# A gated linear attention kernel: two neighbouring tokens in one partition for q, k and v, and half-size TensorE tiles inside a chunk

## The chip, the core and the metric

The kernel runs on one core of a Trainium2 chip. Its time is the device time of one execution in microseconds (us). Before the change three runs took 190.23 to 192.36 us, with a median of 191.33.

## What is computed

Inputs are q, k, v and a complex gate a = a_re + i a_im, each of 4 batches, 8 heads, 768 steps and 48 channels in 32-bit floats. In every head a complex state S of 48 x 48 is carried over the steps, and the result goes through a small two-layer network with a residual:

```python
mag = np.sqrt(a_re * a_re + a_im * a_im)
a_n = a * np.minimum(mag, 0.999) / (mag + 1e-06)     # complex
for t in range(768):
    S = a_n[t][:, None] * S + k[t][:, None] * v[t][None, :]
    y[t] = q[t] @ S.real
x  = y of all 8 heads side by side                   # (4, 768, 384)
xn = (x - mean) / sqrt(var + 1e-6) * g_ln
out = x + relu(xn @ w_ch1) @ w_ch2                   # 384 -> 1536 -> 384
```

## The kernel before

The steps of a batch are cut into chunks of 128. Two neighbouring chunks are a pair; there are 3 pairs a batch and 12 in all (P = 0 to 11, chunk n = 2P + c). Only the first pair (PARTS) is worked on in two parts of four heads each, to start sooner.

For each pair the gates give decays and phases. ScalarE takes ln of a_re (`ln`), its reciprocal (`iv`), VectorE or GpSimd the ratio a_im / a_re (`r`), its square (`r2`); then ln(1 + r2) (`u`), the log magnitude (`l`), its cap (`lc`), and arctan of the ratio (`th`). TensorE sums log magnitudes and phases over the steps with triangular matrices (`dec` L477, `ph` L492/L496), ScalarE makes exponentials (`e`, `en`) and sines and cosines (`sin`, `cos`; `qt` or `abs` give the quarter turn). So k is divided and q multiplied by the running decay (`ke`, `qe`), and each is turned by the phase (`ks`, `qs`, with the cosine part in channels 0 to 47 and the sine part in 64 to 111 of 128).

Then, in each chunk and for each of the 8 heads:

- `kT`, `qT` (L594): transposes of ks and qs, on TensorE with a copy to SBUF (`ksT`, `qsT`), or as a DMA transpose on the SP queue (L599), as the plan says.
- `am` (L617): the scores, `ksT` times `qsT`, 128 x 128; `atm` masks them on VectorE.
- `gm` (L645, with the carried state in L641): ks times v is added to the state; `G` reads it out.
- `y` (L667, L670): masked scores times v, plus qs times the state before the chunk. `x` copies it out of PSUM.

The network follows: `xtr`/`xT` transpose x (L688), `mm1` (L722) multiplies with w_ch1 in six groups a pair, `relu` (L739, L741) reads them out, `mm2` (L754) multiplies with w_ch2, `oa` (L760) and `ot` (L767, L770) scale by 1/std and add x, `st` (L777) stores. The mean and g_ln are folded into w_ch1 at the start (`wp`, `wc`, L388).

In DRAM a chunk's q, k and v lie with one step in a partition, so each packet of a load is one head's 48 channels, 192 bytes (L404). The gates lie with two neighbouring steps in a partition, 384 bytes a packet (L445):

```python
in_=ap[b].rearrange("h (c p) d -> p c h d", p=C)[:, pp * R + c]               # q, k, v: one chunk
in_=ap[b][hs].rearrange("h (k p j) d -> p k h (j d)", p=C, j=R)[:, pp]        # gates: one pair
```

The order of the work is written out: a string PLAN lists every step with its engine (P TensorE, A ScalarE, V VectorE, G GpSimd, S the SP queue) and PSUM bank, and each engine takes its own in that order. An `@` makes a GpSimd step wait for a named VectorE step. `warm` (L787) are 134 matmuls without use that fill the time in which TensorE would wait in the beginning. `tab` are the loads of ScalarE's function tables.

Of the kernel before, what the change touches and what calls it, by code (L numbers as in the profile page):

```python
# [34 lines left out]

ENGINES = {"P": "PE", "A": "ACT", "V": "DVE", "G": "POOL", "S": "SP"}
# [3 lines left out]
aim.0.0:A tab.log.0:A aim.0.1:A ue:G are.0.0:S are.0.1:S pad.e.1:G uth:V one:G warm.0:P0 pad.ks.0:G warm.1:P0  # L40
warm.2:P0 pick:G warm.3:P0 are.1.0:S warm.4:P0 warm.5:P0 warm.6:P0 k.0.1:S ln.0.0:A warm.7:P0 car0.1:G warm.8:P0
cmean:G iv.0.0:A warm.9:P0 ident:G warm.10:P0 warm.11:P0 r.0.0:V warm.12:P0 warm.13:P0 warm.14:P0 aim.1.0:S warm.15:P0
warm.16:P0 warm.17:P0 ln.0.1:A warm.18:P0 warm.19:P0 r2.0.0:A warm.20:P0 k.0.0:S warm.21:P0 warm.22:P0 warm.23:P0
warm.24:P0 u.0.0:A warm.25:P0 warm.26:P0 warm.27:P0 warm.28:P0 iv.0.1:A warm.29:P0 l.0.0:V warm.30:P0 are.2.0:S
warm.31:P0 warm.32:P0 ln.1.0:A warm.33:P0 warm.34:P0 r.0.1:G warm.35:P0 lc.0.0:V warm.36:P0 warm.37:P0 aim.2.0:S
warm.38:P0 warm.39:P0 warm.40:P0 iv.1.0:A warm.41:P0 warm.42:P0 pad.ks.1:G warm.43:P0 warm.44:P0 warm.45:P0 warm.46:P0
warm.47:P0 zdec:G r2.0.1:A warm.48:P0 pad.e.0:G warm.49:P0 pad.qs.0:G warm.50:P0 q.0.1:S warm.51:P0 warm.52:P0 u.0.1:A
warm.53:P0 warm.54:P0 r.1.0:V warm.55:P0 dec.0.0:P0 warm.56:P1 warm.57:P1 q.1.0:S e.0.0:A0 warm.58:P1 warm.59:P1
warm.60:P1 r2.1.0:V warm.61:P1 en.0.0:A0 warm.62:P1 warm.63:P1 warm.64:P1 l.0.1:V warm.65:P1 u.1.0:A warm.66:P1
warm.67:P1 warm.68:P1 warm.69:P1 lc.0.1:V warm.70:P1 are.3.0:S warm.71:P1 warm.72:P1 warm.73:P1 ln.2.0:A warm.74:P1  # L50
l.1.0:V warm.75:P1 warm.76:P1 warm.77:P1 warm.78:P1 dec.0.1:P6 q.1.1:S warm.79:P0 warm.80:P0 lc.1.0:V en.0.1:A6
warm.81:P0 warm.82:P0 warm.83:P0 warm.84:P0 q.0.0:S iv.2.0:A warm.85:P0 warm.86:P0 ke.0.1.0:G@lc.1.0 warm.87:P0
dec.1.0:P0 e.0.1:A6 r.2.0:V wl.1:G warm.88:P2 warm.89:P2 e.1.0:A0 warm.90:P2 warm.91:P2 warm.92:P2 warm.93:P2
warm.94:P2 gln:S r2.2.0:V en.1.0:A0 qrow:G dps.1:P4 dps.0:P5 ke.0.0.0:V warm.95:P2 warm.96:P2 u.2.0:A warm.97:P2
warm.98:P2 decc.1:V4 warm.99:P2 vf.0.0:S car0.0:G warm.100:P2 warm.101:P2 warm.102:P2 mask:G warm.103:P2 warm.104:P2
aim.3.0:S tab.trig.1:A warm.105:P2 warm.106:P2 warm.107:P2 wl.0:G qe.1.0.1:V warm.108:P2 warm.109:P2 vf.0.1:S
warm.110:P2 warm.111:P2 warm.112:P2 qe.1.0.0:V warm.113:P2 warm.114:P2 pad.qs.1:G warm.115:P2 warm.116:P2 l.2.0:V
th.0.0:A warm.117:P2 warm.118:P2 wl.2:G warm.119:P2 ph.0.0:P1 th.0.1:A th.1.0:A qe.0.0.0:V ph.0.1:P4 qe.0.1.0:V
warm.120:P0 warm.121:P0 warm.122:P0 k.1.0:S car.0.0:V1 decc.0:V5 sin.0.0:A1 lc.2.0:V sin.0.1:A4 qt.0.0:P1 ks.0.0.1:V
warm.123:P0 car.0.1:A4 wgc:V cos.0.0:A1 qt.0.1:P4 ph.1.0:P6 k.1.1:S ks.0.1.1:V cos.0.1:A4 qs.0.1.1:V th.2.0:A  # L60
qs.0.0.1:V qs.0.1.0:V wp.1:P5 ks.0.1.0:V sin.1.0:A6 qs.0.0.0:V ks.0.0.0:V qT.1:P4 wc.1.2:V5 tab.log.2:A qT.0:P1
qsT.1:V4 kT.1:P0 qs.1.0.1:G@wc.1.2 dec.2.0:P2 car.1.0:V6 ln.3.0:A warm.124:P4 qsT.0:V1 warm.125:P4 wp.0:P4 e.2.0:A2
are.4.0:S wc.1.0:V5 kT.0:P1 en.2.0:A2 vf.1.0:S ksT.1:V0 ksT.0:A1 wc.0.0:V4 vf.1.1:S am.1:P2 warm.126:P0 wc.1.1:V5
iv.3.0:A warm.127:P0 am.0:P0 wc.0.2:V4 qt.1.0:P6 tab.trig.3:A warm.128:P5 warm.129:P5 warm.130:P5 warm.131:P5
wc.0.1:V4 warm.132:P5 warm.133:P5 atm.0:V0 ph.2.0:P4 r.3.0:G@wc.0.1 cos.1.0:A6 k.2.0:S v.0:A wp.2:P6 atm.1:V2
aim.4.0:S sin.2.0:A4 gm.0:P7 ke.1.0.0:G y.0:P0 G.0:V7 k.2.1:S x.0:A0 qt.2.0:P4 ke.1.0.1:V gm.1:P7 cos.2.0:A4 y.1:P1
q.2.0:S qs.1.0.0:V xtr.0:P0 ks.1.0.0:V x.1:A1 qT.2:P3 th.3.0:A ks.1.0.1:V qT.3:P5 qsT.2:V3 xtr.1:P1 q.2.1:S xT.0:A0
r2.3.0:G@ks.1.0.1 kT.3:P4 qsT.3:A5 xT.1:V1 kT.2:P2 ksT.3:V4 mm1.0.0.0:P0 G.1:V7 q.3.1:S tab.log.4:A v.1:G am.3:P4
ksT.2:V2 mm1.0.0.1:P0 are.5.0:S ke.2.0.0:G atm.3:V4 ln.4.0:A mm1.0.1.0:P2 q.3.0:S wl.3:G mm1.0.1.1:P2 relu.0.0:A0
# [144 lines left out]
def kernel(  # L214
# [60 lines left out]
    def eng(name):  # L275
        return g.ops[name].eng
# [547 lines left out]
```

## Time and profile before

| what | value |
|---|---|
| three runs, median | 191.33 us |
| the profiled execution, own time | 192.75 us |
| its span, first to last instruction | 191.0 us, granted clock 0.995 |
| PE busy (TensorE matmuls) | 177.3 us |
| ACT busy (ScalarE) | 158.9 us |
| DVE busy (VectorE) | 156.6 us |
| POOL busy (GpSimd) | 105.5 us |
| DMA packets | 133,080, of these 127,168 under 512 bytes |
| matmuls on PE | 2045 |

In the profile PE stands for TensorE, PEld for its weight loads, ACT, DVE and POOL for ScalarE, VectorE and GpSimd. SPq, ACTq are an engine's queue while it issues a DMA. A row of the timeline has start, length, engine, line, operation and tiles; a row of the groups has count, busy time, mean length of one and the idle time just before. A matmul's length contains its way through the array, so neighbours overlap.

### The profile page before, as it was taken

The numbers are of one execution on the slowest core, as the hardware profiler recorded it, in microseconds if no ns is written. First come the engines' busy times: TensorE is split into PE (matmuls) and PEld (weight loads), VectorE is DVE, ScalarE is ACT, GpSimd is POOL, SyncE is SP. The second block draws the span as 40 slices with busy tenths as digits, with TensorE's granted clock in tenths as the row PEclk, the third lists the DMA queues.
The fourth block names the chain that finished last, engine by engine and source line by source line (L and its number), as shares of the span: only waits on it lengthen the run. The fifth ranks groups of instructions, "written<-read, shape, count | busy, mean of one in ns | idle before, by whom it ended". The sixth has DMA issues, their size and how long they took to land.

```text
span 191.0 us, 5154 instructions
## 1 busy us (share of the span) xinstructions
PE 177.3 (93%) x2045; PEld 138.6 (73%) x2045; DVE 156.6 (82%) x285; ACT 158.9 (83%) x224; POOL 105.5 (55%) x124
## 2 busy tenths in 40 slices
PE   5999398999999999999968999999999999998992
PEld 3888365788667887776847687877867777786781
DVE  1678699999999999999996998998989867666532
ACT  3989499999999997899949999998999979662340
POOL 7419032579196899071539483347785954940130
PEclk9999999999999999999999999999999999999998
DMA  6999999999969999889999999999799979994032
GB/s 153 278 240 202 212 198 204 210 214 207 242 108 287 205 220 234 154 183 234 136 265 234 190 221 230 282 223 204 141 160 262 217 126 179 256 191 151 5 124 82
DMA packets 133080, 37.57 MB, mean 197 GB/s; under 512 B 127168, under 2 KB 133056, under 8 KB 133056
## 3 DMA queue, kind: packets, MB, share of 16 engines
q1 hardware_dynamic: 107760, 27.21, 70.6%
q10 hardware_dynamic: 22512, 7.67, 18.0%
q0 software_dynamic: 2784, 2.36, 7.9%
q8 instruction: 16, 0.26, 0.6%
q14 instruction: 8, 0.07, 0.1%
HBM read 28.31 MB, written 4.72 MB: 173 GB/s over the span
## 4 chain that ended last, share of the span: by engine, by line
PE 63%; DVE 10%; ACT 9%; DMA 8%; issue 4%; ACTq 2%; POOL 1%; SPq 1%; DVEq 0%; POOLq 0%
PE banks L754 22%; PE banks L722 16%; PE banks L617 5%; PE banks L594 4%; DMA q<-in_q_dram 4%; DMA ksT<-ks 3%; PE banks L477 3%; PE banks L667 2%; ACTq L777 2%; PE banks L496 2%; PE banks L670 2%; DVE w1b L388 2%; DMA are<-in_a_re_dram 2%; PE banks L645 2%; PE banks L688 2%
## 5 line engine op out<-in xcount | busy, mean ns | idle before, releaser
L754 PE MATMUL banks<-w2b,h 128*128 128x384 bf16 (+1 forms) x300 | 55.7, 319 | 0.6 <-ACT h L739 0.6
L722 PE MATMUL banks<-xT,w1b 128*128 128x256 bf16 x432 | 50.9, 272 | 0.7 <-ACT h L739 0.5
L722 PEld LDWEIGHTS <-w1b 128*128 128x128 bf16 x432 | 41.4, 98 | 7.0 <-issue 1.2
L754 PEld LDWEIGHTS <-h 128*128 128x128 bf16 x300 | 26.7, 97 | 13.8 <-ACT h L739 1.0
L295 DVE TENSOR_TENSOR atm<-banks,mask 128x1024 bf16<-128x1024 f32 x24 | 29.0, 1219 | 3.8 <-PE banks L617 2.9
L739 ACT ACTIVATE h<-banks 128x1024 bf16<-128x1024 f32 (+1 forms) x26 | 25.7, 1009 | 4.6 <-DVE ks L295 2.6
L792 ACT ACT_TABLE_LOAD x19 | 24.4, 1283 | 2.6 <-PEq L808 1.3
L295 POOL TENSOR_TENSOR ke<-k,en 128x384 bf16<-128x384 f32 x17 | 15.4, 916 | 14.1 <-ACT e L481 4.3
L767 POOL TENSOR_TENSOR ot<-ot,x 128x384 f32<-128x384 f32 x13 | 12.5, 967 | 14.2 <-ACT ot L760 12.9
L295 POOL TENSOR_TENSOR r<-aim,are 128x768 f16<-128x768 f32 (+1 forms) x8 | 13.7, 1715 | 11.0 <-DVE w1b L388 4.1
L787 PE MATMUL banks<-u_e 128*128 128x256 f16 x134 | 17.5, 286 | 2.2 <-POOL u_e L323 2.2
L295 POOL TENSOR_TENSOR qs<-qe,trig 128x768 bf16<-128x768 bf16 x8 | 13.0, 1640 | 10.3 <-DVE w1b L388 7.2
L617 PE MATMUL banks<-qsT,ksT 128*128 128x128 bf16 x192 | 14.5, 219 | 2.8 <-ACT h L739 2.1
L787 PEld LDWEIGHTS <-u_e 128*128 128x128 f16 x134 | 13.5, 102 | 4.5 <-POOL u_e L323 1.9
L617 PEld LDWEIGHTS <-ksT 128*128 128x128 bf16 x192 | 12.1, 97 | 5.1 <-issue 2.8
L741 DVE TENSOR_SCALAR h<-banks 128x1024 bf16<-128x1024 f32 (+1 forms) x11 | 12.7, 1166 | 2.7 <-PE banks L722 2.7
L295 POOL TENSOR_TENSOR qe<-q,e 128x384 bf16<-128x384 f32 x12 | 11.0, 917 | 6.8 <-DVE r L295 3.6
L466 DVE SCALAR_TENSOR_TENSOR l<-r,w 128x768 f16<-128x768 f16 (+1 forms) x13 | 12.6, 969 | 1.3 <-ACT r L462 1.1
L680 DVE BATCH_NORM_STATS2 stats<-x 128x6 f32<-128x384 bf16 x24 | 13.1, 546 | 0.1
L667 PE MATMUL banks<-v,atm 128*128 128x48 bf16 x192 | 12.0, 183 | 0.0
L514 ACT ACTIVATE trig<-banks 128x768 bf16<-128x768 int16 (+1 forms) x13 | 9.8, 761 | 2.5 <-DVE car L509 2.4
L496 PE MATMUL banks<-th,u_th 128*128 128x384 f16 (+1 forms) x52 | 11.8, 313 | 0.0
(93 smaller groups left out, 380.8 us busy)
## 6 DMA issues: line engine op xcount, KB each, us to landing
k<-in_k_dram SPq DMA_DIRECT2D x24, 192.0 KB, 5.1
q<-in_q_dram SPq DMA_DIRECT2D x24, 192.0 KB, 4.3
are<-in_a_re_dram SPq DMA_DIRECT2D x11, 384.0 KB, 5.1
aim<-in_a_im_dram SPq DMA_DIRECT2D x11, 384.0 KB, 5.0
out_dram<-ot ACTq DMA_DIRECT2D x19, 192.0 KB, 3.4
vf<-in_v_dram ACTq DMA_DIRECT2D x18, 192.0 KB, 4.3
w1b<-in_moe_w_ch_dram POOLq DMA_DIRECT2D x3, 384.0 KB, 7.6
vf<-in_v_dram SPq DMA_DIRECT2D x6, 192.0 KB, 7.0
```

The source lines that it names most:

```text
L295: {"DVE": nc.vector, "POOL": nc.gpsimd}[eng(name)].tensor_tensor(**kw)
L466: nc.vector.scalar_tensor_tensor(out=S_("l"), in0=S_("r2"), scalar=0.5, in1=S_("w"), op0=ALU.mult, op1=ALU.add)
L496: nc.tensor.matmul(heads(ps[:, c]), lhsT=u_th[:, c, j], rhs=step(T("th", P), j), start=False, stop=(j == R - 1), skip_group_check=True)
L617: nc.tensor.matmul(ps[:, h], lhsT=T("ksT", n)[:, h], rhs=T("qsT", n)[:, h], start=True, stop=True)
L667: nc.tensor.matmul(ps[:, h], lhsT=T("atm", n)[:, h], rhs=T("v", P)[:, c, h], start=True, stop=nfirst)
L680: nc.vector.bn_stats(out=T("stats", n), in_=T("x", n))
L722: nc.tensor.matmul(ps[:, jj], lhsT=w1b[:, dc, ts(gi * JG + jj, C)], rhs=T("xT", P)[:, dc].rearrange("p c t -> p (c t)"), start=(dc == 0), ...
L739: act(out=dst, in_=src, func=AF.Relu)
L741: nc.vector.tensor_scalar(out=dst, in0=src, scalar1=0.0, scalar2=None, op0=ALU.max)
L754: nc.tensor.matmul(bank(own)[:, 0:w], lhsT=T("h", P)[:, j, ts(c, C)], rhs=w2b[:, j, es], start=(j == 0), stop=(j == NJ - 1))
L787: g.add(f"warm.{i}", lambda i=i: nc.tensor.matmul(bank(f"warm.{i}")[:, 0:256], lhsT=u_e[:, 0, 0], rhs=u_e[:, 1].rearrange("p j t -> p (j t ...
L792: g.add(f"tab.{nm}.{i}", lambda tab=tab: nc.scalar.preload_act_table_set(tab))
```

## The change

q, k and v are loaded as the gates are: one load a pair, two neighbouring steps j = 0, 1 in a partition, 384 bytes a packet. A chunk of 128 steps is then 64 partitions x 2 steps, and the two chunks of a pair are the lower and the upper 64 partitions. With that:

- The tiles of scores hold four heads of both chunks (`n = 2P + m`, m the half of the heads). `am` has, for every head and key step j, two matmuls of 64 weight columns, one for each chunk, into PSUM partitions 0 to 63 and 64 to 127.
- `gm` and the local part of `y` take 64 rows at a time, one matmul for each j. `y` is one step a pair, in two banks.
- The triangular matrices, the mask and the stores follow the new order of steps. Two stores a pair, one for each j; the last pair's are cut finer. `ot` holds a pair (3 buffers of it, not 5 of a chunk).
- In the first pair the log magnitude comes from are^2 + aim^2 (`sa`, `sb`, `sc`, DIRECT), no longer by way of the ratio.
- PLAN is new. `warm` goes from 134 to 55. Steps that change their place: xT 16 on VectorE, 8 on ScalarE -> 2, 2 and 20 as DMA transposes on SP; ksT 14 -> 21 and qsT 11 -> 0 on SP; all loads of v and all stores on SP (ACT issued 39 DMAs, then 1; SP 110, then 133); table loads 19 -> 21.

```diff
-        for c in range(R):
-            for nm, ap in (("k", k), ("q", q), ("vf", v)):
-                add(f"{nm}.{P}.{c}", lambda nm=nm, ap=ap, c=c: ring(f"{nm}.{P}.{c}").dma_start(
-                    out=T(nm, P)[:, c],
-                    in_=ap[b].rearrange("h (c p) d -> p c h d", p=C)[:, pp * R + c]),
-                    uses=[(nm, P)])
+        def load(name, tile, ap, hs):
+            ring(name).dma_start(out=tile[:, hs], in_=ap[b][hs].rearrange(
+                "h (k p j) d -> p k h (j d)", p=C, j=R)[:, pp])
...
+            if direct:
+                add(f"u.{X}", lambda S_=S_, sq=sq: act(out=S_("r2"), in_=sq[:, 0], func=AF.Ln,
+                                                       scale=1.0 + 2.0 * LNEPS),
+                    needs=[f"sc.{X}"], uses=[("r2", P)])
...
             def f_am(n):
                 ps = bank2(f"am.{n}").rearrange("p s (h t) -> p (s h) t", t=C)
-                for h in range(H):
-                    nc.tensor.matmul(ps[:, h], lhsT=T("ksT", n)[:, h], rhs=T("qsT", n)[:, h],
-                                     start=True, stop=True)
+                for h in range(HH):
+                    for j in range(R):
+                        for c in range(R):
+                            nc.tensor.matmul(ps[ds(c * HALF, HALF), h * R + j],
+                                             lhsT=T("ksT", n)[:, h, j, ds(c * HALF, HALF)],
+                                             rhs=T("qsT", n)[:, h, c], start=True, stop=True)
...
+        def f_y():
+            ps = [heads(banks[:, g.bank[f"y.{P}"] + c, 0:DM]) for c in range(R)]
+            for h in range(H):
+                for j in range(R):
+                    for c in range(R):
+                        nc.tensor.matmul(
+                            ps[c][:, h],
+                            lhsT=T("atm", n0 + h // HH)[ds(c * HALF, HALF), h % HH, j],
+                            rhs=vj(c, h, j), start=(h == 0 and j == 0),
+                            stop=(j == R - 1 and first and c == 0), skip_group_check=True)
+            for c in range(1 if first else 0, R):
+                for h in range(H):
+                    nc.tensor.matmul(ps[c][:, h], lhsT=T("qsT", n0 + h // HH)[:, h % HH, c],
+                                     rhs=T("G", n0 + c - 1)[:, h], start=False, stop=True,
+                                     skip_group_check=True)
...
                     for h in range(H):
-                        nc.tensor.matmul(heads(ps)[:, h], lhsT=T("ks", P)[:, c, h],
-                                         rhs=T("v", P)[:, c, h], start=nfirst, stop=True,
-                                         skip_group_check=True)
+                        for j in range(R):
+                            nc.tensor.matmul(heads(ps)[:, h],
+                                             lhsT=T("ks", P)[ds(c * HALF, HALF), h, j],
+                                             rhs=vj(c, h, j), start=nfirst and h == 0 and j == 0, stop=True,
+                                             skip_group_check=True)
...
+        if P < NP - 1:
+            for j in range(R):
+                add(f"st.{P}.{j}", lambda j=j: ring(f"st.{P}.{j}").dma_start(
+                    out=rows_out(j), in_=T("ot", P)[ds(j * HALF, HALF)]),
+                    needs=[f"ot.{P * R}", f"ot.{P * R + 1}"], uses=[("ot", P)])
...
-    for i in range(134):
+    for i in range(55):
```

More of the change, by code (lines that the diff above doesn't have):

```diff
@@ L58 @@
[L58 to L67, printed above, removed]
@@ new lines @@
+G.8:A3 gm.9:P3 car.6.0:A0 mm2.7.1:P2 are.9.0:S qe.6.0.0:V ke.6.0.1:G ks.5.0.0:G abs.6.0:V0 atm.9:V6 q.7.0:S aim.9.0:S
+cos.6.0:A y.4:P6 th.7.0:A ph.7.0:P0 G.9:V3 relu.3.2:A4 vf.6.0:S st.0.0:S l.7.0:V qT.10:P4 x.8:V6 mm2.6.0:P3 qsT.10:V4
+car.7.0:V0 v.6:G@l.7.0 aim.8.0:S abs.7.0:V0 ks.6.0.1:V st.0.1:S mm2.7.2:P2 xT.8:S x.9:A6 bn.9:V xT.9:S qT.11:P6
+sin.7.0:A0 qsT.11:V6 ks.6.0.0:G tab.log.12:A iv.8.0:A mm2.6.1:P3 mm2.6.2:P3 ot.6:V3 st.1.1:S r.8.0:G ksT.10:S lc.7.0:V
+ln.9.0:A iv.9.0:A vf.5.0:S mm1.4.2.0:P4 mm1.4.1.1:P0 mm1.4.2.1:P4 mm1.4.1.0:P0 oa.7:A2 bn.8:V mm1.4.0.0:P6
@@ L742, in f_relu @@
                                                 op0=ALU.max)
-                add(name, f_relu, needs=[f"mm1.{P}.{gi}.{x}" for x in ((s,) if end else (0, 1))],
+                add(name, f_relu, needs=[f"mm1.{P}.{gi}.{x}" for x in ((s,) if end else (0, 1))]
+                    + ([f"u.0.{i}" for i in range(PARTS[0])] if P == 1 else []),
                     uses=[("h", P)], ps=(o, 2))
```

427 lines of the change are left out of this document (229 added, 198 removed), and 2 rows, old and new, of the table RINGS.

## The prediction

> **What bounds the kernel now.** I read the page first, then the engines by stages, the waits of TensorE, and the order of single matmuls.
>
> ```profile
> span 191.0 us, 5154 instructions
> ...
> PE 177.3 (93%) x2045; PEld 138.6 (73%) x2045; DVE 156.6 (82%) x285; ACT 158.9 (83%) x224; POOL 105.5 (55%) x124
> ...
> PE 63%; DVE 10%; ACT 9%; DMA 8%; issue 4%; ACTq 2%; POOL 1%; SPq 1%; DVEq 0%; POOLq 0%
> ```
>
> PE is busy 93% of the span, and 63% of the chain that ended last is PE's own work. ACT (83%) and DVE (82%) come next, so the stages have to be looked at singly (columns: PE, weight loads, DVE, ACT, POOL busy, granted clock, DMA share, GB/s):
>
> ```profile
> 20.00:30.00 10.00, 6.44 (x63) 4.28 (x62) 8.89 (x24) 7.53 (x12) 1.64 (x1) 1.00 1.12 209
> ...
> 40.00:50.00 10.00, 10.00 (x133) 8.57 (x131) 9.57 (x17) 9.73 (x14) 7.13 (x9) 1.00 1.20 228
> ...
> 60.00:70.00 10.00, 10.00 (x155) 8.47 (x154) 9.76 (x17) 9.69 (x16) 9.37 (x8) 1.00 1.05 223
> ...
> 110.00:120.00 10.00, 10.00 (x134) 8.02 (x132) 8.96 (x15) 9.52 (x14) 5.88 (x6) 1.00 1.15 223
> ...
> 180.00:190.00 10.00, 7.21 (x67) 5.88 (x64) 3.50 (x7) 2.88 (x7) 2.70 (x3) 0.96 0.29 100
> 190.00:191.00 1.00, 0.00 (x0) 0.00 (x0) 0.00 (x0) 0.00 (x0) 0.00 (x0) 0.50 0.00 0
> ```
>
> From 35 us on PE is at 10.00 of 10 in nearly every stretch, at full clock, with ACT and DVE at 9.5 to 9.7 beside it. Only the first 35 us and the last 8 belong to others; the last row shows the clock at 0.50 once PE has stopped. What PE still waits for in between:
>
> ```profile
> PE banks L617 <- ACT h L739: 2.1, 1, 2.1
> PE banks L617 <- DVE ksT L292: 0.6, 1, 0.6
> PE banks L754 <- ACT h L739: 0.6, 1, 0.6
> PE banks L722 <- ACT h L739: 0.5, 1, 0.5
> ...
> PE banks L722 <- ACT sh L531: 0.2, 1, 0.2
> ```
>
> That is 4.0 us in all. So behind 35 us the time is a sum of PE instruction slots, and the questions are how many slots the change adds and how much earlier PE's dense work can start. The price of a slot is the distance between two starts, not a duration:
>
> ```profile
> 65.27 0.33 PE L688 MATMUL banks<-ident,x 128*128 128x128 bf16 x3
> 65.44 0.19 PE L667 MATMUL banks<-v,atm 128*128 128x48 bf16 x1
> ...
> 65.82 0.18 PE L670 MATMUL banks<-G,qsT 128*128 128x48 bf16 x1
> 65.90 1.05 PE L617 MATMUL banks<-qsT,ksT 128*128 128x128 bf16 x16
> ```
> ```profile
> 15.64 0.55 PE L573 MATMUL banks<-ident,e 128*128 128x1 bf16 x16
> ```
> ```profile
> 60.48 0.45 PE banks L617 x8
> 60.93 0.65 PE banks L754 x4
> ...
> 121.39 3.27 PE banks L722 x30
> ```
>
> Sixteen matmuls of 48 columns start between 65.44 and 65.82, 25 ns apart, though each lasts 183 ns. The sixteen of one column (15.64) are (0.55 - 0.16) / 15 = 26 ns apart: with 1 column as with 48 an instruction costs a slot of 25 ns, however little it streams. Eight of 128 columns take 0.45 us, 56 ns each; thirty of 256 take 3.27 us, 109 ns each. Where the shape changes (three transposes from 65.27, then 48 columns at 65.44, exactly 3 x 56 ns later) nothing is lost.
>
> **The change part by part.** The plans and the built program give these counts of PE instructions.
>
> ```profile
> L617 PE MATMUL banks<-qsT,ksT 128*128 128x128 bf16 x192 | 14.5, 219 | 2.8 <-ACT h L739 2.1 <-DVE ksT L292 0.6
> ...
> L667 PE MATMUL banks<-v,atm 128*128 128x48 bf16 x192 | 12.0, 183 | 0.0
> ...
> L645 PE MATMUL banks<-v,ks 128*128 128x48 bf16 x160 | 7.2, 183 | 0.0
> L688 PE MATMUL banks<-ident,x 128*128 128x128 bf16 x72 | 7.1, 219 | 0.0
> ...
> L787 PE MATMUL banks<-u_e 128*128 128x256 f16 x134 | 17.5, 286 | 2.2 <-POOL u_e L323 2.2
> ```
>
> (1) Transposes. On PE there are 256 (184 of ks and qs, 72 of x) and then 228 (216 and 12), since 20 of 24 x tiles and 21 of 24 ks tiles now go through the DMA and every qs tile comes back to PE: -28 x 56 ns = **-1.6 us**.
>
> (2) State product (L645). 160 matmuls of 128 rows become 320 of 64 rows. All of one step use the same half of the array's rows, so they cannot sit side by side; each takes its 25 ns slot: 160 x 25.3 ns = **+4.0 us**. Less than nothing is excluded, since no column is saved.
>
> (3) Local output (L667). 192 matmuls of 128 rows become 384 of 64 rows, alternating between the upper and the lower half and between two banks. Bounds: 0, if the two of a pair share a slot, and 192 x 25.3 ns = 4.9 us. No row shows two in one slot, and the one-column row says the slot is paid per instruction, so I take **+4.9 us**. One y now serves both chunks and waits for both score tiles; the first x waits for the second with it, which the head's term (6) contains.
>
> (4) Score product (L617). 192 matmuls become 384 with half the weight columns, each still streaming 128 columns. Bounds: 0, if the two halves (array columns 0 to 63 and 64 to 127, issued in turn) stream together, and 192 x 56 ns = 10.7 us if they follow one another. Two slots of 25 ns fit into 56 ns, so the slot does not speak against a pair here, and the halves share no cell: I take **0** and keep 10.7 for the range.
>
> (5) Changes of tile size. The built order of PE changes between 128x128, 128x64 and 64x128 tiles 102 times; the kernel before never does. Bounds: 0, as at 65.44 where only the shape changes, and a full emptying of the array, 183 - 25 = 158 ns each, 16.1 us. The nearest row is the one that loses nothing; I add one slot for the change, 102 x 25.3 ns = **+2.6 us**.
> The Trainium skill, TensorEngine Tiling (Array Packing), section Tiling Modes, says that a change of tiling mode drains the engine. By that rule the term would be the 16.1 us of the far end; no trace so far has such a change, and it is the second rival below. The same section lets different tiles load and multiply in parallel, which would make (3) and (4) both 0.
>
> (6) The head. x of the first chunk decides when PE's dense work starts:
>
> ```profile
> 4.20 0.52 ACT L448 ACTIVATE w<-are 128x384 f32<-128x384 f32 x1 [1.60 <-DMA are<-in_a_re_dram]
> ...
> 22.39 0.87 ACT L514 ACTIVATE trig<-banks 128x384 bf16<-128x384 int16 x2 [2.39 <-DVE car L509]
> ...
> 34.64 0.48 ACT L290 CAST x<-banks 128x384 bf16<-128x384 f32 x1
> ```
> ```profile
> L792 ACT ACT_TABLE_LOAD x19 | 24.4, 1283 | 2.6 <-PEq L808 1.3 <-issue 0.9
> ...
> L448 ACT ACTIVATE w<-are 128x768 f32<-128x768 f32 x11 | 9.4, 850 | 0.0
> ...
> L290 ACT COPY ksT<-banks 128x1024 bf16<-128x1024 bf16 x1 | 1.0, 1015 | 0.0
> ```
> ```profile
> 13.77 7.08 DMA q<-in_q_dram
> ```
>
> Between the first load (4.20) and the first cast of x (34.64) ACT does 18 half-size and 18 full activations, three table loads and a ksT copy; it waits 2.4 us at 22.39 and 0.7 us in two smaller gaps. After the change its order has 16 halves, 15 full ones, five table loads and one more carry: -2 x 0.52 - 3 x 0.85 - 1.0 + 2 x 1.28 + 0.5 = -1.5 us. The first pair's q load, which held the chain for 7.08 us, now has two tokens and 384 bytes in a packet, and its log magnitude comes straight from are and aim (DIRECT), no longer behind ln, reciprocal and ratio. So x.0 may come up to 1.5 + 3.1 = 4.6 us earlier. Against it: 79 fill-ins go (79 x 109 ns = 8.6 us of slots in time that PE waits anyway). They cost nothing while the clock stays at 1.00; if it falls to the 0.50 of the last window's row, the roughly 4 us of first-pair matmuls on this chain take twice as long (an estimate: 32 transposes and 16 scores at 56 ns, sums and outputs at their slots). Bounds -4.6 to +4.0; I take **-2.0 us**.
>
> (7) ACT's issue queue. All but one of its 39 DMA issues move to SP. ACT's own work stays (two table loads, three output scalings, a ReLU and r2 more; four |phase|, six xT copies, three G less: about +1 us), DVE loses some 5 us, POOL gains 12 of its 85 idle, all by the plans' counts times the grouped rows' means. The gain is bounded by PE's 4.0 us of waits and by nothing on the other side; I take **-1.5 us**.
>
> (8) DMA and SP, costed at nothing:
>
> ```profile
> DMA packets 133080, 37.57 MB, mean 197 GB/s; under 512 B 127168, under 2 KB 133056, under 8 KB 133056
> ...
> q1 hardware_dynamic: 107760, 27.21, 70.6%
> ```
> ```profile
> ksT<-ks SPq DMA_TRANSPOSE x14, 4.7
> ```
> ```profile
> L292 DVE COPY xT<-banks 128x384 bf16<-128x384 bf16 x16 | 5.4, 351 | 3.5 <-PE banks L688 3.5
> ```
>
> q, k and v drop from 72 x 1024 packets to half. At 0.706 x 16 x 191 us / 107,760 = 20 ns a packet that frees up to 36,864 x 20 / 16 = 46 us of DMA time, but DMA is only 8% of the chain, half of it the head's q load, already in (6). SP issues 133 instead of 110, each new x transpose behind loads, stores and other transposes; a store of a pair waits for both chunks' outputs, and in SP's order aim of pair 8, the pair's other store and x transposes 8 and 9 stand behind the first of them, so ACT's ln and r of pair 8 and mm1 of pair 4 would wait with it. A transpose lands 4.7 us after its issue, against some 0.7 us for PE transpose and copy. What waits is mm1 of that pair; older pairs' mm2 groups (0.65 us each) stand in front of it in PE's order. Without that cover it is 4 us a pair, up to 40 us for ten pairs. In the tail six such groups (3.9 us) just cover the last two.
>
> Sum: -1.6 + 4.0 + 4.9 + 0 + 2.6 - 2.0 - 1.5 = **+6.4 us**. The profiled execution took 192.75 us (span 191.0, 1.75 outside), 1.4 above the median of the three, 191.33. The profiled one would become 199.2, and a median run **197.8**, rounded to 198.
>
> **The rivals.**
> *Faster: the half tiles share the array and changes of size are free.* Then (3), (4) and (5) vanish, PE grows by only 4.0 - 1.6 = 2.4 us, and the starved stretches decide: the head at its full 4.6 and ACT's relief at its full 4.0 give -6.2 us, **185**. For it: each pair is issued back to back with no common cell. Against: no row shows a shared slot. It decides once terms (2) to (5) together stay below 8.3 us: 8.6 of head and relief, plus the 1.6 of (1), less the 1.9 of one per cent.
> *Slower: each change of size empties the array.* (5) at 16.1 instead of 2.6: **211**. For it: 102 changes in the densest stretch; against: at 65.44, where only the shape changes, no gap is seen.
> *Slower: score halves one after another.* (4) at 10.7: **208.5**.
> *No change.* The packets are halved but PE neither gains nor loses: half tiles cost about 5 us and head plus queue give them back, **191**. For it: (6) and (7) can hold 8.6 us.
>
> **How the numbers follow.** Forecast 0.40 (198, its own range 193 to 204), faster 0.26, emptying 0.18, score halves 0.08, no change 0.08. Over 1% is about what a measurement of this kernel tells from no change: faster 0.26, within 1% 0.08, slower 0.40 + 0.18 + 0.08 = 0.66. The range must reach into both sides: 185 holds about half of the faster case, 212 nearly all of the emptying; what lies beyond (two slow terms at once, 222, or x transposes uncovered) is the rest.
>
> **What would show it.** In the profile after: starts of the 64-row matmuls in y 25 ns apart (3 right) or in pairs (wrong); score groups of 16 halves in 0.45 us (4 right) or 0.9 (wrong); a gap ahead of each half-tile group of 25 ns (5 right) or about 160 (second rival). x.0 near 32.5 us (6). PE at 10 of 10 from 35 us on; if instead mm1 waits for x transposes, (8) was wrong. A time below 190 makes the forecast wrong, above 206 one of the prices.

## The result, and the profile after

Four runs of the changed kernel took 213.63 to 218.95 us, median **216.0 us**; four of the kernel before in the same session had a median of 191.21. The ratio is **1.125 (1.113 to 1.138)**: 24 us slower, where 6.4 were forecast. Ratios in this document compare undisturbed runs alone, so they need not be the quotient of two medians.

The profiled execution took 215.4 us. Its page, the rows that answer to those of before:

```profile
span 213.7 us, 6014 instructions
...
PE 184.9 (87%) x2482; PEld 134.7 (63%) x2482; DVE 159.9 (75%) x268; ACT 161.9 (76%) x220; POOL 121.8 (57%) x137
...
PE 46%; DVE 22%; DMA 16%; ACT 6%; SPq 4%; issue 4%; DVEq 0%; ACTq 0%
...
DMA packets 99819, 38.53 MB, mean 180 GB/s; under 512 B 93904, under 2 KB 99792, under 8 KB 99792
```

PE is busy for 185 us, 7.6 more than before, but in a span 22.7 us longer: its share falls from 93% to 87%, and in the chain that ended last from 63% to 46%. DVE has 22% of that chain where it had 10, DMA 16% where it had 8. The packets fell by a quarter, so the loads did become coarser. The engines by stages (PE, weight loads, DVE, ACT, POOL, granted clock, DMA share, GB/s):

```profile
20.00:30.00 10.00, 8.94 (x129) 6.32 (x130) 9.59 (x20) 9.90 (x12) 8.41 (x13) 1.00 1.16 293
40.00:50.00 10.00, 8.58 (x137) 6.14 (x133) 9.23 (x13) 7.19 (x10) 6.69 (x8) 1.00 1.18 238
60.00:70.00 10.00, 9.73 (x174) 6.99 (x172) 9.53 (x19) 9.35 (x13) 7.56 (x6) 1.00 1.15 251
110.00:120.00 10.00, 9.06 (x118) 6.03 (x116) 8.40 (x14) 9.45 (x13) 9.76 (x11) 1.00 0.82 203
...
210.00:213.00 3.00, 0.00 (x0) 0.00 (x0) 0.00 (x0) 0.00 (x0) 0.00 (x0) 0.53 0.18 42
```

Before, PE stood at 10.00 in the three middle stretches; now it idles 1.42 us at 40, 0.27 at 60, 0.94 at 110, while DVE and ACT are not fuller than they were. Short gaps between the starts of matmuls, as those at changes of size below, are not in these idle times: a matmul's length reaches over them. The clock is at 1.00, so none of this is a slower TensorE; the last row (0.53) only has PE stopped. What PE waits for:

```profile
PE banks L527 <- ACT th L515: 5.9, 2, 3.2
PE banks L657 <- DMA ksT<-ks: 3.8, 3, 1.6
PE banks L778 <- DMA xT<-x: 2.8, 3, 1.4
```

The first row lies in the head. The second and third are new: score and mm1 groups wait 6.6 us for transposes that the DMA makes. Before, these two DMA rows did not exist. The order of single matmuls, in one stretch that holds all the half-size shapes:

```profile
38.85 0.64 PE L657 MATMUL banks<-qsT,ksT 128*64 128x128 bf16 x16 [0.87 <-DMA ksT<-ks]
39.42 0.34 PE L703 MATMUL banks<-G,ident 128*128 128x384 bf16 x1
39.69 0.57 PE L708 MATMUL banks<-v,ks 64*128 64x48 bf16 x16
40.19 0.64 PE L657 MATMUL banks<-qsT,ksT 128*64 128x128 bf16 x16
40.76 0.34 PE L522 MATMUL banks<-car,pick 128*128 128x384 f16 x1
...
41.75 0.81 PE L383 MATMUL banks<-w1b,gc 128*128 128x512 bf16 x3
42.49 0.57 PE L680 MATMUL banks<-v,atm 64*128 64x48 bf16 x32
43.00 0.58 PE L687 MATMUL banks<-G,qsT 128*128 128x48 bf16 x16
43.42 0.81 PE L778 MATMUL banks<-xT,w1b 128*128 128x256 bf16 x6
```

Read as the prediction did, by distances between starts. The sixteen score halves start (0.64 - 0.22) / 15 = 28 ns apart, so a pair takes the 56 ns of one whole matmul. The sixteen of the state product (39.69) start 25.8 ns apart, a slot each. The 32 of the local output (42.49) start (0.57 - 0.18) / 31 = 12.6 ns apart, two in one slot. And each change of tile size leaves a gap: the halves from 38.85 are through at 38.85 + 16 x 0.028 = 39.30, the next starts at 39.42; its 384 columns take 0.163, the next starts at 39.69 and not 39.58; 16 slots later, at 40.10, PE is free, and 40.19 is the next start. The gaps are 0.12, 0.11 and 0.09 us. Where size stays and only the shape changes, from L687 to L778, sixteen slots lead from 43.00 to 43.42 with no gap.

The difference of the spans, 22.7 us, divides by two marks on PE, the first mm1 and the last mm2 group. Before and after:

```profile
38.10 0.82 PE L722 MATMUL banks<-xT,w1b 128*128 128x256 bf16 x6
```
```profile
183.12 4.09 PE L754 MATMUL banks<-w2b,h 128*128 128x384 bf16 x36
```
```profile
36.51 1.47 PE L778 MATMUL banks<-xT,w1b 128*128 128x256 bf16 x12
```
```profile
203.89 4.09 PE L811 MATMUL banks<-w2b,h 128*128 128x384 bf16 x36
```

The first mm1 is 1.6 us sooner. Behind the start of the last mm2 group 7.9 us were left and now 9.8. The dense stretch between the marks went from 145.0 to 167.4 us, **+22.4**, and the tail has +1.9. The question is what filled the dense stretch.

### The profile page after: what moved, and what is told of

Its sections match the earlier page's. It is cut to its first block, busy times and chain, and to the rows that moved or that the text cites. A ratio compares the mean times of both kernels' runs of the same rounds, so it can differ in the third digit from the quotient of the medians.

```text
span 213.7 us, 6014 instructions
## 1 busy us (share of the span) xinstructions
PE 184.9 (87%) x2482; PEld 134.7 (63%) x2482; DVE 159.9 (75%) x268; ACT 161.9 (76%) x220; POOL 121.8 (57%) x137
## 4 chain that ended last, share of the span: by engine, by line
PE 46%; DVE 22%; DMA 16%; ACT 6%; SPq 4%; issue 4%; DVEq 0%; ACTq 0%
PE banks L778 14%; PE banks L811 11%; DMA ksT<-ks 8%; PE banks L657 5%; PE banks L708 4%; DVE atm L288 4%; PE banks L631 3%; DMA q<-in_q_dram 3%; DMA xT<-x 3%; SPq L402 3%; DVE l L495 2%; PE banks L680 2%; PE banks L527 2%; PE banks L687 2%; DVE ke L288 2%
## 5 line engine op out<-in xcount | busy, mean ns | idle before, releaser
L778 PE MATMUL banks<-xT,w1b 128*128 128x256 bf16 x432 | 52.7, 273 | 4.5 <-DMA xT<-x 2.8
L811 PE MATMUL banks<-w2b,h 128*128 128x384 bf16 (+1 forms) x300 | 52.3, 320 | 0.0
L778 PEld LDWEIGHTS <-w1b 128*128 128x128 bf16 x432 | 40.5, 98 | 13.0 <-issue 4.3
L795 ACT ACTIVATE h<-banks 128x1024 bf16<-128x1024 f32 (+1 forms) x27 | 27.1, 1008 | 12.4 <-PE banks L778 12.1
L288 POOL TENSOR_TENSOR qs<-qe,trig 128x768 bf16<-128x768 bf16 (+1 forms) x13 | 22.0, 1700 | 6.2 <-DVE qe L288 5.9
L824 POOL TENSOR_TENSOR ot<-ot,x 128x384 f32<-128x384 f32 x16 | 14.7, 933 | 14.0 <-ACT ot L817 13.3
L288 POOL TENSOR_TENSOR r<-aim,are 128x768 f16<-128x768 f32 (+1 forms) x8 | 14.1, 1759 | 14.1 <-ACT h L795 8.5
L657 PE MATMUL banks<-qsT,ksT 128*64 128x128 bf16 x384 | 15.0, 221 | 5.3 <-DMA ksT<-ks 3.8
L657 PEld LDWEIGHTS <-ksT 128*64 128x64 bf16 x384 | 11.7, 109 | 9.6 <-DMA ksT<-ks 5.0
L288 POOL TENSOR_TENSOR qe<-q,e 128x384 bf16<-128x384 f32 x14 | 13.5, 969 | 7.5 <-ACT e L511 5.6
L285 DVE COPY qsT<-banks 128x1024 bf16<-128x1024 bf16 x20 | 13.2, 683 | 2.0 <-PE banks L631 1.9
L631 PE MATMUL banks<-ident,qs 128*128 128x128 bf16 x192 | 14.0, 219 | 0.5 <-POOL qs L288 0.4
L708 PEld LDWEIGHTS <-ks 64*128 64x128 bf16 x320 | 9.4, 93 | 6.3 <-issue 4.6
L817 ACT ACTIVATE ot<-banks,rstd 128x384 f32<-128x384 f32 x16 | 8.9, 578 | 5.7 <-issue 3.0
```

Of the source, the lines that this page charges most:

```text
L285: nc.vector.tensor_copy(out=dst, in_=src)
L288: {"DVE": nc.vector, "POOL": nc.gpsimd}[eng(name)].tensor_tensor(**kw)
L631: nc.tensor.transpose(dst, T(nm, P)[:, hm][:, h, j], ident)
L657: nc.tensor.matmul(ps[ds(c * HALF, HALF), h * R + j], lhsT=T("ksT", n)[:, h, j, ds(c * HALF, HALF)], rhs=T("qsT", n)[:, h, c], start=True, ...
L708: nc.tensor.matmul(heads(ps)[:, h], lhsT=T("ks", P)[ds(c * HALF, HALF), h, j], rhs=vj(c, h, j), start=nfirst and h == 0 and j == 0, stop=True,
L778: nc.tensor.matmul(ps[:, jj], lhsT=w1b[:, dc, ts(gi * JG + jj, C)], rhs=T("xT", P)[:, dc].rearrange("p c t -> p (c t)"), start=(dc == 0), ...
```

## The experiments

Three theories stood against each other. **A**: the changes of tile size cost about 0.1 us each, some 10 us together. **B**: the added DMA transposes hold PE, by arriving late and by what they do to SP's queue. **C**: something else in the new order (an engine overloaded, the stores, the fewer fill-ins). Times are medians; "before" beside them is 190.7 to 191.8 in every session.

### Full-size tiles, and where the DMA transposes are not used (e1, e2, e3)

e1 puts every half-size matmul of the changed kernel on a 128 x 128 tile with as many slots as before, e2 replaces the DMA transposes by VectorE copies, e3 does both.

```diff
# e1: am, y, gm on whole tiles
-  nc.tensor.matmul(ps[ds(c * HALF, HALF), h * R + j], lhsT=T("ksT", n)[:, h, j, ds(c * HALF, HALF)], ...)
+  nc.tensor.matmul(ps[:, h * R + j], lhsT=T("ksT", n)[:, h, j], rhs=T("qsT", n)[:, h, j], ...)
-  lhsT=T("atm", n0 + h // HH)[ds(c * HALF, HALF), h % HH, j], rhs=vj(c, h, j)      # for j, for c
+  lhsT=T("atm", n0 + h // HH)[:, h % HH, c], rhs=T("v", P)[:, h, ds(c * D, D)]     # for c
-  lhsT=T("ks", P)[ds(c * HALF, HALF), h, j], rhs=vj(c, h, j)
+  lhsT=T("ks", P)[:, h, j], rhs=T("v", P)[:, h, ds(j * D, D)]
# e2 (and e3, on top of e1): copies of the same tiles on VectorE
-  nc.sync.dma_start(out=T("xT", P)[:, :, c], in_=T("x", n), transpose=True)         # ksT alike
+  nc.vector.tensor_copy(out=T("xT", P)[:, :, c], in_=T("x", n).rearrange(...))
```

> The changed kernel with every half-size matmul put back to a 128x128 tile that streams the same columns in the same number of PE slots: one full matmul for each pair of score halves and of output halves, 128 rows in place of 64 in the state product. It leaves the split of the two chunks out of scores, outputs and state, so only its time counts. Theory A (each of the 102 changes of tile size costs about 0.11 us, the gap seen around the half-size groups in the changed kernel's timeline): 102 x 0.11 = 11 us less, about 205 us. Theory B (the pace is set by tiles transposed by DMA behind one queue, and PE has the time to change sizes): less than 3 us off, 213 or more, with PE's waits on ksT and xT grown by what the changes took.

> The changed kernel with its 41 DMA transposes replaced by plain VectorE copies at the same places of the order; it leaves the transposition of those tiles out. Theory A: PE's direct waits on ksT (3.8 us) and xT (2.8 us) go, so 6 to 7 us less, about 209 us. Theory B: also the waits that these pass on to ACT and DVE go, 12 us less or more, 204 us or below. If VectorE's added copies (41 of some 0.3 to 0.7 us) become the bound, no gain or a loss.

> Both together: full-size tiles and VectorE copies in place of DMA transposes, with the same parts left out. Theory A and B agree that both costs are gone; if they add up, 216 - 11 - 7 = 198 us. A rest well above 198 is the new order itself; near 191 or below, the two causes explain all of the loss and the head may even gain.

**e1: 207.13 us**, ratio 1.083 (1.078 to 1.089), 8.1 us under the changed kernel by the ratios and 9.0 by the spans (204.7 against 213.7). Its timeline of the same stretch:

```profile
38.38 0.62 PE L656 MATMUL banks<-qsT,ksT 128*128 128x128 bf16 x8 [0.40 <-DMA ksT<-ks]
38.83 0.33 PE L699 MATMUL banks<-G,ident 128*128 128x384 bf16 x1
39.00 0.56 PE L704 MATMUL banks<-v,ks 128*128 128x48 bf16 x16
39.40 0.61 PE L656 MATMUL banks<-qsT,ksT 128*128 128x128 bf16 x8
...
41.47 0.56 PE L677 MATMUL banks<-v,atm 128*128 128x48 bf16 x16
41.88 0.56 PE L683 MATMUL banks<-G,qsT 128*128 128x48 bf16 x16
42.28 0.82 PE L774 MATMUL banks<-xT,w1b 128*128 128x256 bf16 x6
```

Eight whole matmuls lead from 38.38 to 38.83 at 56 ns, no gap behind them. The same work up to the same mm1 group takes 42.28 - 38.38 = 3.90 us, and 43.42 - 38.85 = 4.57 in the changed kernel: 0.67 us more for six changes, **0.11 us each**. The page agrees:

```profile
PE 175.0 (86%) x2098; PEld 134.1 (65%) x2098; DVE 159.1 (78%) x268; ACT 160.8 (79%) x220; POOL 121.5 (59%) x137
```

For the same slots PE is busy 175.0 us and not 184.9, since the lengths of matmuls cover the gaps: 9.9 us of the changed kernel's busy PE are no work. Theory A holds, at 10 to 11 us for 102 changes by the trace and 8 to 9 in time. That the difference falls into time in which PE would wait anyway is likely, but not shown.

**e2: 226.91 us**, 1.189 (1.181 to 1.197), and **e3: 222.08**, 1.162 (1.155 to 1.168). Both were to show theory B as a gain, and became slower by 11 to 15 us. The groups of VectorE in e2, and its chain that ended last, say why:

```profile
L636 DVE COPY ksT<-ks 128x1024 bf16<-128x1024 bf16 x21 | 14.2, 679 | 3.8 <-POOL half_n L311 3.6
...
L745 DVE COPY xT<-x 128x384 bf16<-128x384 bf16 x20 | 6.4, 338 | 2.0 <-ACT x L283 2.0
```
```profile
PE 38%; DVE 30%; POOL 10%; issue 8%; ACT 8%; DMA 3%; SPq 0%; DVEq 0%; POOLq 0%; ACTq 0%
```

The copies take 20.6 us of an engine that was 75% busy, and its share of the chain grows from 22% to 30, GpSimd's from nothing to 10. So e2 and e3 say nothing of B. That e3 is 4.8 us under e2 agrees with A.

### One kind of half tile in the kernel before (e4)

```diff
-  nc.tensor.matmul(ps[:, h], lhsT=T("ksT", n)[:, h], rhs=T("qsT", n)[:, h], ...)
+  for c2 in range(2):
+      nc.tensor.matmul(ps[ds(c2 * HALF, HALF), h], lhsT=T("ksT", n)[:, h, ds(c2 * HALF, HALF)],
+                       rhs=T("qsT", n)[:, h], ...)
```

> The kernel before with one part of the change alone: each score matmul as two of 64 weight columns, into the lower and the upper 64 partitions; all else as before. 48 changes of tile size or a few less. Theory A: 47 x 0.11 = 5 us more, 196 us, while each pair still takes 56 ns. If the halves followed one another, 11 us more on top. If a change cost only an issue slot of 25 ns, 1.2 us more, 192.5.

**193.81 us**, 1.013 (1.009 to 1.018): +2.6 us for 46 changes into and out of half-size scores (two of the 24 groups follow each other directly).

```profile
59.51 0.49 PE L496 MATMUL banks<-th,u_th 128*128 128x384 f16 x2
59.93 0.64 PE L618 MATMUL banks<-qsT,ksT 128*64 128x128 bf16 x16
60.50 0.82 PE L756 MATMUL banks<-w2b,h 128*128 128x384 bf16 x4
```

Two slots of 163 ns behind 59.51 end at 59.84, the halves start at 59.93; they end at 60.38, the next starts at 60.50: 0.09 + 0.12 us for a pair of changes, 23 x 0.21 = 4.8 us. Half of that reaches the end; PE's waits had 4.0 us to give. The price of a change is thus the same in the other kernel, and the pair of halves is free there too.

### Not waiting for the transposes, and not making them (e5, e6, e7, e16)

e5 lets mm1 stream a constant tile and the scores load one in place of xT and ksT, so PE no longer depends on the DMA transposes, which still run. It relieves more than that: mm1 then waits for no x at all and the scores for no ks, however these are transposed. e6 is e5 with the whole tiles of e1. e16 is e6 with the transposes not issued. e7 goes the other way: the kernel before with 20 of its xT moved from TensorE to SP, nothing else.

```diff
# e5 (e6: on e1)
-  rhs=T("xT", P)[:, dc].rearrange("p c t -> p (c t)")
+  rhs=mask.rearrange("p c t -> p (c t)")
-  lhsT=T("ksT", n)[:, h, j, ds(c * HALF, HALF)]
+  lhsT=ident[:, ds(c * HALF, HALF)]
# e16, on e6: the two nc.sync.dma_start(..., transpose=True) are left out
# e7, in the PLAN of the kernel before, for 20 tiles
-  xtr.6:P1  xT.6:V1
+  xT.6:S
```

> The changed kernel in which mm1 streams a constant tile (the mask, 256 columns) and the score matmuls load a constant (the identity) in place of xT and ksT: every DMA transpose is still issued and still runs, but no matmul waits for one. It leaves x and ks out of those products. Theory A (size changes plus direct waits): PE's waits on ksT (3.8 us) and xT (2.8 us) go, about 209 us. Theory B (late transposes hold up the chain beyond PE's own waits): 12 us or more off, 204 or below. Theory C (the new order itself is slow, whoever delivers the tiles): less than 3 us off, 213 or more.

> The same with full-size tiles, so neither size changes nor waits on DMA transposes; left out are the split of the chunks, and x and ks in those products. With the full-size run at 207.1: theory A 207 - 7 = 200, theory B 195 or below, theory C 204 or above. What is left above 191 is state-product slots (4.0 us), less 1.6 us of transposes, and the order.

> The kernel before with the same 20 x tiles transposed by DMA from SP as after the change, at the places where its plan has the copy; all else as before. PE saves 60 slots of 56 ns (3.4 us), DVE and ACT the copies. If the latency is hidden by mm2 groups, as the prediction had it: 188 to 191. If SP's queue and the landing time hold up mm1 also here: 195 or more.

> Full-size tiles, no matmul waiting for a DMA transpose (203.9 us), and now the 41 DMA transposes are not issued at all; their tiles stay unwritten and unread. If they still cost through SP's queue (1.2 to 1.3 us of issue each, with loads of the gates, k and q behind them), 3 us less or more, 201 or below. If not, 203.9, and the rest is no matter of the SP queue.

**e5: 212.31**, 1.121 (1.108 to 1.134): 3.7 us under the changed kernel by the medians, 0.8 by the ratios, and the intervals overlap, so it shows no clear gain. **e6: 203.88**, 1.076 (1.071 to 1.082), 1.3 us under e1 by the ratios, 2.9 by the spans, and so at the 204 of its theory C: not waiting brings little. **e16: 200.48**, 1.048 (1.041 to 1.055), 6.7 us under e1 by the ratios, 6.3 by the spans. So the DMA transposes together cost at most **6.3 to 6.7 us**. At most 1.3 to 2.9 of it is PE's waiting for them (and for x and ks as such); the step from e6 to e16, 3.4 us by the spans and 5.4 by the ratios, is what they cost when no matmul waits for one. How it divides is less sure than the sum.

What that second part is, the pages of e6 and then e16 show:

```profile
L288 POOL TENSOR_TENSOR r<-aim,are 128x768 f16<-128x768 f32 (+1 forms) x8 | 13.8, 1727 | 13.7 <-DMA aim<-in_a_im_dram 8.7
```
```profile
L288 POOL TENSOR_TENSOR r<-aim,are 128x768 f16<-128x768 f32 (+1 forms) x8 | 13.7, 1714 | 8.1 <-ACT are L451 8.1
```

In e6 GpSimd stands idle 8.7 us for one load of aim. That load is issued at 130.67, right behind two ksT transposes that take SP from 126.64 to 130.62, and the chain that ended last runs through the second of them, the load (4.1 us) and GpSimd's r. In e16 GpSimd waits for no load behind the head. The loads themselves land no faster there: from issue to landing the medians of are, aim, q, k and v are 4.7 to 5.7 us in e6 and 4.8 to 5.6 in e16. So it is the later issue, and not the transposes' own traffic, that makes them late. This is read in e6; in the changed kernel other waits come last at that place (GpSimd's r waits 8.5 us for a ReLU of ScalarE), and its waits for loads behind the head are 4.5 us for v and 1.8 for q.

**e7: 229.44 us**, 1.211 (1.197 to 1.225), +38 us by the medians and +40 by the ratios:

```profile
PE banks L619 <- DMA xT<-x: 31.8, 10, 8.4
```

PE waits 31.8 us for xT, 8.4 in one place. In an order of SP that was not written for them the x transposes come late: the one that PE waits longest for is issued at 45.62, behind loads that SP issues without a pause, and lands 7.4 us later, where the median of the 20 is 2.8. The changed kernel's own order keeps this small, but not at zero. Its SP queue (start, length of the issue), two steps of the chain that ended last, and the two groups of PE that they release:

```profile
44.03 1.18 SPq L747 DMA_TRANSPOSE xT<-x  x1
...
81.67 5.52 SPq L636 DMA_TRANSPOSE ksT<-ks  x2
```
```profile
81.67 6.43 DMA ksT<-ks
...
158.28 3.92 DMA xT<-x
```
```profile
88.15 0.64 PE L657 MATMUL banks<-qsT,ksT 128*64 128x128 bf16 x16 [1.63 <-DMA ksT<-ks]
```
```profile
162.33 0.81 PE L778 MATMUL banks<-xT,w1b 128*128 128x256 bf16 x6 [1.42 <-DMA xT<-x]
```

One issue of an x transpose of 128 x 384 occupies SP for at least 1.18 us (median 1.20), nearly as long as one of ksT of 128 x 1024 (at least 1.23, median 1.32). Some take longer: the two of ksT from 81.67 keep SP for 5.52 us, and a load of are follows only at 87.28. Summed over the single issues, SP spends 63 us on issuing 41 transposes; before it was 38 us for 25. SP also stands still ahead of a transpose whose tile is not ready yet, 47 us in all (33 before). Yet all its issues together take 141 us, and 132 before, because the loads became fewer: SP is not fuller, but more of its work has to wait for the engines. The chain runs 6.43 us through the ksT that was issued at 81.67 and 3.92 through the xT of 158.28, and at the end of these PE stands still for 1.63 and 1.42 us.

### The local output's order (e9)

```diff
-  for h in range(H):
-      for j in range(R):
-          for c in range(R):            # lower and upper rows in turn, two banks
+  for c in range(R):                    # one half of the rows after the other
+      for h in range(H):
+          for j in range(R):
```

> The changed kernel with the loop over the two chunks moved outermost in the local output: all 16 matmuls of the lower 64 partitions, then all 16 of the upper ones; same instructions, same results, same changes of tile size. If two neighbours on different row halves share a slot (in the changed kernel 32 of them take 0.58 us), they now cannot: 16 x 25 ns more in each of 12 outputs, 4.9 us more, about 220 us, and 32 starts 25 ns apart. If the 12.6 ns have another reason, no change.

**219.4 us**, 1.146 (1.139 to 1.154), +4.0 on the changed kernel.

```profile
66.42 0.90 PE L681 MATMUL banks<-v,atm 64*128 64x48 bf16 x32
```

The 32 start (0.90 - 0.18) / 31 = 23 ns apart and not 12.6: 12 x 0.33 = 4.0 us, as measured. The sharing is real, and it is the alternation that makes it. The loop alternates two things, the halves of the rows and the two PSUM banks; the banks alone do not do it, since e1 alternates them too with whole tiles and its sixteen (at 41.47 above) start (0.56 - 0.18) / 15 = 25 ns apart.

### SP's and ACT's queues, fill-ins (e8, e10, e15)

```diff
# e8, PLAN of the kernel before, 18 loads of v and 19 stores
-  vf.3.0:A  st.0:A
+  vf.3.0:S  st.0:S
# e10: 55 of the 134 warm, evenly left;  e15: both
```

> The kernel before with all stores and all loads of v issued from SP, as after the change; ACT issues only two loads. Prediction's step on ACT's issue queue: up to 4 us less (187), its value 1.5 us less. If SP's order is what suffers (a store that waits holds up the loads behind it): 193 or more.

> The kernel before with 55 of its 134 fill-ins, spread evenly over the same places; all else as before. In the changed kernel the first matmuls run 0.22 us apart at 256 columns until some 13 us. If the fill-ins kept the clock up and the clock matters for the head: 1 to 3 us more. If PE only waits there: 191.

> The kernel before with stores and loads of v from SP and 55 of 134 fill-ins, the two single steps that gave 189.4 and 189.8 us. If they add up, about 188 us, faster than both kernels; if both gain from the same stretch of the head, 189.5.

**e8: 189.35 us**, 0.994 (0.989 to 0.999). **e10: 189.81**, 0.993 (0.989 to 0.998). **e15: 190.63**, 0.996 (0.991 to 1.000). By the ratios, relief of ACT's queue is worth 1.1 us in the kernel before, and the smaller number of fill-ins does no harm, rather the opposite; the two gains do not add up. e8 and e10 do the whole computation and are some 0.6% faster than the kernel before.

### What is left: an engine, or the tail (e11 to e14, e17)

e16 still stands 9 us above the kernel before by the medians (7.4 by the spans, since the profiled execution of before lies 1.5 us over its median). These five start from e6, in which the DMA transposes still run, and lighten one engine, all three, or the tail.

```diff
# e11: qs of pairs 5 to 7, POOL -> DVE        -  qs.6.0.0:G           +  qs.6.0.0:V
# e12: three of the last six stores           -  st.23.0.0:S          +  st.23.0.0:A
# e13: DVE, half of atm and of qsT's copies  -  out=T("atm", n)      +  out=T("atm", n)[:, :, 0]
# e14: ACT and DVE, half of each full relu    -  js = ts(gi, JG)      +  js = ds(gi * JG, 2)
# e17: all of e13 and e14, and eight qs POOL -> DVE
```

> The run with full-size tiles and no waits on DMA transposes (203.9 us), with five products of the phase (qs of pairs 5 to 7, 1.6 us each) moved from GpSimd to VectorE (0.55 us each); the same parts left out as there. Around 98 to 110 us that run's chain goes through GpSimd's r, v and qs while PE is busy only 7.5 and 8.4 of 10. Theory C1 (the new order loads GpSimd at a place where others wait): 2 us less or more, 202 or below. Theory C2 (VectorE and ACT are the bound there): no gain, or 1 to 3 us more.

> The same base (203.9 us) with three of the last six stores issued from ACT. Each chunk of the last pair now has one store for every step of two, and SP issues them one after another, 0.6 us each; the time from the last output to the end is 5.3 us in the changed kernel and 3.1 us before. If the queue is why: 1.2 to 1.8 us less, about 202.4. If it is the stores' own landing time: 203.9.

> Full-size tiles and no waits on DMA transposes (203.9 us), and in addition half of the masking and half of the copies of transposed tiles left out, about 20 us less work on VectorE (24 x 0.6 + 23 x 0.33 us). The longest waits of PE in that run are for VectorE (qsT 2.5 us, atm 1.5). If VectorE is what the new order starves PE with: 4 us less or more, 200 or below. If ScalarE or the order's dependencies are: within 1 us of 203.9.

> The same base (203.9 us) with half of each ReLU left out (37 x 0.5 us, 27 of them on ScalarE, 10 on VectorE). If ScalarE is what starves PE: 4 us less or more. If neither this nor the lighter VectorE moves it, the idle time lies in the order itself, not in one engine's load.

> The same base (203.9 us) with all three reliefs at once: half the masking and half of the copies of transposed tiles, half of each ReLU left out, and qs of pairs 4 to 7 and 9 on VectorE instead of GpSimd. If several engines together starve PE (each alone did nothing): 4 us less or more, 200 or below. If not, the waits come from the order's own dependencies and from PE's added work.

Beside e6's 203.88 they took **203.18, 204.69, 204.26, 204.05 and 205.99 us** (ratios 1.061, 1.069, 1.072, 1.069, 1.075 beside 1.076). In the profiles of e6, e11, e12, e13, e16 and e17 the granted clock is 0.50 for 3.4 to 6.8 us between 17 and 26 us, in the changed kernel's it is not, so a difference of about a microsecond among them is not read. e11's interval, 1.053 to 1.069, lies just under e6's: it is 2.9 us lower by the ratios, but 0.7 by the medians, and e17, which contains its five moves and three more, is not lower than e6. So GpSimd's part stays open between nothing and 3 us. The others recover at most 1.3 us. Beside DMA transposes that hold up the loads, then, neither VectorE's nor ScalarE's load nor the queue of the last stores holds the time; whether lighter engines would gain on top of e16 was not run. What e16's marks say of it:

```profile
36.57 1.47 PE L772 MATMUL banks<-mask,w1b 128*128 128x256 bf16 x12
```
```profile
189.10 4.09 PE L805 MATMUL banks<-w2b,h 128*128 128x384 bf16 x36
```

First mm1 at 36.57 (1.5 us sooner than before), last mm2 group at 189.10, span 198.4: the dense stretch is 152.5 us, +7.5, and the tail 9.3, +1.4. Of the +7.5, 2.4 are slots (160 of the state product more, 28 transposes fewer). About 2 are work that PE did ahead of its first mm1 before and does behind it now: counted by slots, without fill-ins, 14.1 us and 12.1. The remaining 3 are what is left over, presumably waits scattered over the new order, and with the tail's 1.4 they stay **open**: no run shows which dependence makes them.

## Why the prediction was wrong, step by step

Direction right, size not: 198 forecast, 216 measured, outside the range of 185 to 212. The ledger in us, by the prediction's terms:

| step | forecast | measured | by |
|---|---|---|---|
| (1), (2) transposes, state product | +2.4 | +2.4 | slots of 56 and 25.8 ns in the trace |
| (3) local output | +4.9 | 0 | 12.6 ns apart; e9 puts it back: +4.0 |
| (4) score halves | 0 | 0 | 28 ns apart; e4 the same |
| (5) changes of size | +2.6 | +8.1 to 9.0 | e1 |
| (6) head, with the tail | -2.0 | about +2 | marks in e16: -1.5 start, +2 moved work, +1.4 tail |
| (7) ACT's queue | -1.5 | -1.1 in the kernel before | e8; not seen in this kernel |
| (8) DMA and SP | 0 | +6.3 to 6.7 at most | e16 against e1 |
| the rest | none | about +3 | e16, open |

By the spans the steps from the changed kernel to e1, to e16 and to the kernel before are 9.0 + 6.3 + 7.4 = 22.7 us. The measured column comes near that without (7), but this is no test of it: the last row is the remainder.

**(5) is the term that was mis-sized.** It was taken at a slot, 25 ns, "the nearest row", a place where only the shape changed. That row was not near: it has no change of size at all, and shows nothing of one. The measured 0.11 us lies at two thirds of the far end of 158 ns. The rival of the emptying was right that every change costs, with too high a price; whether the array empties the runs do not show. The Trainium skill, TensorEngine Tiling (Array Packing), section Tiling Modes, has a change of mode drain the engine, and the trace agrees in kind: about 0.1 us is lost at every change of size and nothing at a change of shape.

**(3) failed in the other direction.** The one-column row showed that whole-tile matmuls start no closer than 25 ns. It was taken to hold for two matmuls on different halves of the rows, which no row showed; there the two share a slot, 12.6 ns apart. The same section of the Trainium skill lets different tiles multiply in parallel, and the trace agrees. The errors of (3) and (5) nearly cancel: the PE terms (1) to (5) came to +9.9 in the forecast and to +10.5 to 11.4 as measured. That is luck; neither term was right.

**(8) is the largest part of the miss.** Of the 16.3 us between +6.4 and +22.7, up to 6.7 belong to it, 4 to (6), 1.5 to (7), about 1 to the PE terms, and 3 are open. It was costed at nothing because older mm2 groups stand in front of the waiting mm1. The cover was too thin at the places quoted above, and the second half of the price was not looked at: the issue itself. The prediction's own list of durations had a ksT transpose at 4.7 us from issue to landing, but it left out that each issue keeps SP for more than a microsecond with the loads of later pairs behind it. The prediction did see that a store which waits holds up the loads behind it; that a transpose does so too, it did not. Here the landing is

```profile
ksT<-ks SPq DMA_TRANSPOSE x21, 4.1
xT<-x SPq DMA_TRANSPOSE x20, 2.6
```

and it is not the length that hurts but its place in SP's order. The sign that the prediction named for this, mm1 waiting for xT, is in the waits.

**(6)**: the cast of x.0 did come early, as forecast (near 32.5):

```profile
31.66 0.86 ACT L283 CAST x<-banks 128x384 bf16<-128x384 f32 x2
```
```profile
33.19 0.81 PE L507 MATMUL banks<-l,u_e 128*128 128x384 f16 x4 [0.44 <-DVE l L498]
33.84 0.61 PE L631 MATMUL banks<-ident,ks 128*128 128x128 bf16 x8
...
35.26 1.14 PE L631 MATMUL banks<-ident,qs 128*128 128x128 bf16 x16 [0.43 <-POOL qs L288]
```

It runs at 31.66, where it was at 34.64, 3.0 us sooner. Only 1.6 of it reach mm1. In PE's order the second pair's sums (33.19, waiting for DVE), eight ks and sixteen qs transposes (35.26, waiting for POOL) stand ahead of mm1; that is what is late next, and the prediction stopped at x.0. What PE had not yet done of the first pairs' work it did later, in the dense stretch, so the sooner start bought nothing net. The feared slow TensorE did come, but early and cheaply: its matmuls run at half the pace until 12.2 us, and before only until 4.9 (last section). e10 with as few fill-ins is slow until 6.1 us and again from 10.3 to 12.0, and takes no longer than the kernel before; from 20 us on the clock is at 1.00.

**The rivals.** *Faster* died by (5) and (8), although its half-tile terms (3) and (4) were indeed zero. *Each change empties the array* came nearest with 211, but with 16.1 us for (5) where 8 to 9 were measured, and without (8). *Score halves one after another* did not come. *No change* needed (8) at nothing.

## What to carry to other kernels

Half-size tiles on different halves of the array's rows or columns took no more time here than whole ones when issued in turn, but each switch between sizes cost PE about 0.1 us, so group all work of one size before changing, and count the changes in the built order before counting the slots saved. A transpose moved from TensorE to a DMA costs its place in the issuing queue: price its issue, 1.2 us or more here, and the queue's waiting for its tile, for everything that stands behind it, not only its landing. And a row may stand for a cost only if it contains the thing costed; where no row does, take a middle of the bounds rather than the cheap end.

## What the hardware showed that was not expected

- Two matmuls of 64 rows and 48 columns, on different halves of the rows and in two banks, start 12.6 ns apart (32 in 0.57 us); on the same half one after another 23 to 26 ns.
- A change of tile size costs 0.08 to 0.12 us in every direction seen (128x64, 64x128 and 128x128), in both kernels; the 0.12 is on leaving 128x64.
- The issue of a DMA transpose takes SP at least 1.18 us for 128 x 384 and 1.23 for 128 x 1024, up to 4.2 us for one.
- TensorE's first matmuls run at half the pace: nine of 256 columns take 2.12 us, 0.21 us apart, and from 12.27 on fifteen take 1.80, 0.109 apart. In the kernel before the pace changes at 4.9 us. A window of the profile prints a granted clock of 1.00 from the start, but the trace holds no record of the clock ahead of 12.2 us (4.9 before), so that 1.00 says nothing of this stretch.

```profile
8.58 2.12 PE L851 MATMUL banks<-u_e 128*128 128x256 f16 x9
...
12.27 1.80 PE L851 MATMUL banks<-u_e 128*128 128x256 f16 x15
```
